# Attention, experts and MLP in one kernel: rooms of 240 rows in the wide expert stages, a rewritten end of attention, other pauses between scatters

## The chip, the cores and the metric

The kernel runs on one core of one Trainium2 chip. The time is device time in microseconds (us), from the start to the end of one execution. A profile of one execution gives the rows that are shown below; engines are PE (TensorE, matmuls), PEld (its weight loads), DVE (VectorE), ACT (ScalarE), POOL (GpSimd) and SP (SyncE, which issues most loads).

## The reference

Attention in a window of 64 feeds a mixture of experts, which feeds an MLP. Cut to what matters:

```python
# attention: q, k, v of shape (2, 8, 576, 64); tokens see themselves and 63 before
attn = softmax(q @ k.T / sqrt(64), masked to the window)
x = (attn @ v) as 1152 tokens x 512
# experts: 8 of them, each token goes to one
expert_idx = argmax(x @ w_gate);  gate_w = its probability
for i in range(1152):             # places in order, at most 288 per expert
    if counts[e := expert_idx[i]] < 288: disp[e, counts[e]] = x[i]; counts[e] += 1
y = relu(disp @ w1) @ w2          # 512 -> 1024 -> 512, per expert
out[i] = gate_w[i] * y[expert_idx[i], pos[i]]
# MLP on all 1152 tokens
h = out @ w_in                    # 512 -> 2048
g = max(h, 0) + alpha * min(h, 0)
return g @ w_out                  # 2048 -> 512
```

With the inputs used here the experts get 254, 234, 220, 194, 123, 74, 42 and 11 tokens, in order of size.

## The kernel before, in words

**Precision.** Big products are made from three fast ones. Each float32 operand is split into a high and a low half in the matmul type f32r (11 bits of mantissa): `whi` and `wlo` of the weights, `xh` and `xl` of the data; a product is whi·xh + wlo·xh + whi·xl. ACT makes most `whi` (each fourth is made by DVE), DVE makes all `wlo`. Some small products use plain float32 (`xap`, `aps`, `ay`, `pps`, `py`).

**Attention.** Nine tiles of 128 tokens go through a pipeline that is written out by hand: in turn `t`, PE makes the scores of tile t (`pe_scores`), transposes the probabilities of tile t-1 (`pe_turn`, tile `tp`; `put_turn` copies them out as `ptT`), multiplies them by the values (`pe_values`), and for tile t-2 transposes the result (`pe_columns`) and makes the gate's logits (`pe_logits`, tile `lg`). Engines run their instructions in the order of the code.

**Routing.** Tiles are routed in three batches: b0 is tiles 0 to 3, b1 tiles 4 to 6, b2 tiles 7 and 8. A batch goes through `choosing` (the best expert of each token), `weighing` (its probability), `pe_dispatch` and `dispatching` (each token's row number `sl` in the table), and then one `scatter` per tile: an indirect DMA on POOL that writes 128 rows of 528 words to a table `xe` in HBM, sorted by expert. These small steps on DVE are Python generators; `step(n)` puts n of b0's next steps between the steps of attention. Behind each scatter stand a memset of the tile `spacer` and five memsets of the tile `between`, which pace POOL.

**The star.** After b0 the kernel guesses the largest expert (`choose_star`) and takes the rows that it has so far: DVE makes one-hot matrices (`pick`), PE gathers with them (`pe_ahead`, tile `xap`), and its first 128 rows go through the expert in plain float32 (`go_ahead`: matmuls `aps`, transposes `atp`, matmuls `ay`), while the routing of b2 is under way. After the last scatter, `star_rows` gathers its other rows with one indirect DMA (`sx`). It waits for all scatters, and the stream of weight loads goes on behind it.

**Experts.** Experts are sorted by size, and a place p has the expert of rank `ORDER[p]`, ORDER = (0, 1, 4, 2, 5, 6, 7, 3). Each place has a room, a fixed number of rows:

```python
WIDE, NARROW, HALF = min(cap, 256), 128, 64
room = [WIDE if 1 <= r <= 3 else HALF if r >= 6 else NARROW for r in ORDER]
```

Places 1, 3 and 7 (`HOST`) are wide: tokens are the moving side of the matmul and 128 columns of the weights stand in the array. `wide_up` makes 96 matmuls into `hps`, ACT and DVE turn these into `hh` and `hl`; `wide_down` makes 96 matmuls into `y`, which go out as the halves `x2h`, `x2l`. Places 0, 2 and 4 are narrow: 128 tokens stand in the array and weights move (`sps` and `sy`; `sh`, `sl` and transposes `stp` between). Places 5 and 6 (`PAIR`) have 64 rows each and run in plain float32 between the steps of HOST. What each expert has beyond its room is handled behind a test that these inputs don't reach.

Rows reach the experts by indirect DMAs on POOL (`rows_of`): nine gathers `xg`, two for a wide place, and nine gathers `gt` of the gates.

**Loads.** SP streams weights into tiles `raw` as they come free; `prepare` splits the next weight tile wherever the stages call it. In the HOST stage the first weights of the MLP are converted too (`cvt_tick`: ACT's `mag`, DVE's `w`).

**MLP.** Four rounds, each on a quarter of the hidden columns for three blocks of 384 tokens: matmuls `gps` (384 columns) and `ops` (512 columns), with the PReLU on ACT and DVE between.

Of the kernel before, what the change touches and what calls it, by code (L numbers as in the profile page):

```python
# [27 lines left out]
def attention_moe_mlp_kernel(  # L28
# [27 lines left out]
    room = [WIDE if 1 <= r <= 3 else HALF if r >= 6 else NARROW for r in ORDER]  # L56
# [151 lines left out]
    spacer = const.tile([1, 1], F32, name="spacer")  # L208
# [13 lines left out]
    with tc.manual_schedule():  # L222
# [13 lines left out]
        with ExitStack() as es:  # L236
# [205 lines left out]
            def pe_turn(t):  # L442
                tps[t] = []
                for s in range(2):
                    tps[t].append(ps_t.tile([128, 4, 128], F32, name="tp", tag="tp"))
                    for p in range(4):
                        nc.tensor.transpose(tps[t][s][:, p, :], pts[t][s][:, p, :], identf)  # L447
                    if t == NTILE - 1 and not s:
                        pe_ahead((1,), b0[:2])

            def put_turn(t):
                ptTs[t] = []
                for s in range(2):
                    ptTs[t].append(wk.tile([128, 4, 128], F32, name="ptT", tag="ptT"))
                    (nc.vector.tensor_copy if s and t == NTILE - 1 else nc.scalar.copy)(ptTs[t][s], tps[t][s])
# [327 lines left out]
            def scatter(t, ts, sl):  # L783
# [5 lines left out]
                for _ in range(5):  # L789
# [130 lines left out]
            for t in range(NTILE + 2):  # L920
                if t < NTILE:
                    pe_scores(t)
                    if t < 2:
                        keep_busy(4 - t)
                    peak(t, int(t < NTILE - 1))
                    if t == NTILE - 1:
                        run(*chain)
                if 1 <= t <= NTILE:
                    if t == NTILE:
                        chosen, weights, places = choosing(b1), weighing(b1), dispatching(b1)  # L930
                        some(chosen, 6)
                        some(weights, 2)
                    if t == NTILE:
                        pe_ahead((0,))
                    pe_turn(t - 1)
                    put_turn(t - 1)
                if t == NTILE:
                    run(chosen)
                if t >= 2:
                    if t == NTILE + 1:  # L940
                        pe_ahead((1,), b0[2:])
                    pe_columns(t - 2)
                    put_columns(t - 2)
                if t == NTILE:
                    pe_dispatch(b1)
                    some(places, 8)
                if t < NTILE:
                    softmax(t, HEADS)
                if t == NTILE + 1:
                    pe_ahead((2,))  # L950
                    xa = wk.tile([128, 4, 128], F32, name="axT", tag="ptT")
                    nc.scalar.copy(xa[:, :2], star_x[0][:, :2])
                    run(places)
                    while waiting:
                        scatter(*waiting.pop(0))
                if 1 <= t <= NTILE:
# [3 lines left out]
                if 1 <= t <= NTILE:  # L960
# [3 lines left out]
                if t == NTILE:  # L964
                    run(weights)
                pe_free.append(t)
                step({6: 4, 7: 6}.get(t, 2))
# [3 lines left out]

            choose(b2)
            going = go_ahead()
            pe_ahead((3,))
            nc.scalar.copy(xa[:, 2:], star_x[0][:, 2:])
            pe_dispatch(b2)
            next(going)
            weigh(b2)

# [6 lines left out]
            while waiting:  # L986
                scatter(*waiting.pop(0))
# [30 lines left out]
        with ExitStack() as es:  # L1018
# [6 lines left out]
            def rows_of(dst, src, index):  # L1025
# [3 lines left out]
                for x in scattered:  # L1029
                    tc.add_manual_dep(ins.ins, x.ins.name, mybir.DependencyInfo(  # L1030
                        mybir.DependencyClass.Sync, mybir.DependencyReason.DATA), reason="rows scattered")

            def gather(p):

                for h in range(room[p] // 128 if p not in PAIR else 1):
# [40 lines left out]
            def wide_up(p, xt, between=lambda c: None):  # L1076
                hT, at = [], first_part[p]
                for c in range(4):
                    hi, lo = (w.rearrange("p (k f) -> p k f", k=4) for w in parts.pop(at + c))
                    ps = ps_h.tile([128, 2, WIDE], F32, name="hps", tag="h")  # L1080
                    for f in range(2):
                        fs = slice(128 * f, 128 * f + 128)

                        for n, (i, j) in enumerate(((0, 0), (1, 0), (0, 1))):
                            for kk in range(4):
                                nc.tensor.matmul(ps[:, f, :], (hi, lo)[i][:, kk, fs], xt[j][:, kk, :],  # L1086
# [5 lines left out]
                    hh = hp.tile([128, 2, WIDE], F32R, name="hh", tag="hh")  # L1092
# [467 lines left out]
```

## Time and profile before

| | us |
|---|---|
| median of 3 runs | 408.92 |
| their range | 408.39 to 409.47 |
| the profiled execution's own time | 407.18 |
| its span in the profile | 405.3 |
| mean granted TensorE clock, as a share of full speed | 0.992 |

The profiled execution is one more run, so its own time is not the median; its span runs from the first to the last instruction on the core. A row's durations come from this one execution. Where a row says x24, 24 instructions of a kind are taken together, and the time is theirs from the first start to the last end; matmuls overlap in the array, so the distance between two of them is such a time in the chain divided by the count, not the mean duration of one.

### The profile page before, as it was taken

What the parts mean: (1) busy time and instruction counts of PE and PEld (TensorE: products, weight loads), DVE (VectorE), ACT (ScalarE), POOL (GpSimd) and SP (SyncE); (2) the same over time, 40 slices, a digit from 0 to 9 for tenths busy, and PEclk for the clock granted to TensorE, in tenths of its full rate; (3) what the DMA queues carried; (4) which work ended last, traced back from release to release, by engine and by line L of the source; (5) the groups of instructions that cost most, each with busy time, mean ns of one, the idle gap of its engine ahead of it and who ended that gap; (6) DMA issues with size and microseconds to landing.
All of it is one profiled execution on the core that took longest, in us unless ns stands there. A gap on an engine that the chain in (4) does not pass through costs nothing.

```text
span 405.3 us, 7932 instructions
## 1 busy us (share of the span) xinstructions
PE 388.7 (96%) x2931; PEld 345.9 (85%) x2932; DVE 286.5 (71%) x686; ACT 198.2 (49%) x371; POOL 66.4 (16%) x170
## 2 busy tenths in 40 slices
PE   7999997999999999999999999999999999999991
PEld 4888873999989996877999889998899988999880
DVE  3779797689987765558599866999739972355220
ACT  4979464474563444453377655774127620254000
POOL 5542687010037100000000000000000000000431
PEclk9999999999999999999999999999999999999996
DMA  7761975999997572986323343323401000000221
GB/s 260 243 202 42 352 275 170 394 408 407 342 303 266 181 241 71 341 292 232 107 95 116 109 151 131 129 104 112 149 1 55 0 2 0 0 2 1 81 104 56
DMA packets 20446, 66.12 MB, mean 163 GB/s; under 512 B 2992, under 2 KB 2992, under 8 KB 20400
## 3 DMA queue, kind: packets, MB, share of 16 engines
q1 hardware_dynamic: 17728, 57.74, 40.5%
q0 software_dynamic: 2528, 7.53, 5.1%
q8 instruction: 25, 0.41, 0.4%
q10 hardware_dynamic: 144, 0.26, 0.2%
q14 instruction: 21, 0.17, 0.1%
HBM read 60.74 MB, written 4.79 MB: 162 GB/s over the span
## 4 chain that ended last, share of the span: by engine, by line
PE 87%; DVE 5%; DMA 3%; issue 2%; POOL 1%; ACT 1%; SPq 0%; POOLq 0%
PE gps L220 25%; PE ops L1387 24%; PE y L220 9%; PE hps L1086 7%; PE sps L220 4%; PE sy L220 4%; PE sc L419 2%; PE pps L1254 2%; PE py L1269 2%; PE av L463 2%; PE tp L447 1%; DMA v<-v_in 1%; PE lg L489 1%; DMA sx<-xe,ix 1%; PE xtp L1061 1%
## 5 line engine op out<-in xcount | busy, mean ns | idle before, releaser
L220 PE MATMUL gps<-x2h,wlo 128*128 128x384 f32 x192 | 64.2, 334 | 0.0
L220 PE MATMUL gps<-x2h,whi 128*128 128x384 f32 x192 | 64.2, 334 | 0.0
L220 PE MATMUL gps<-x2l,whi 128*128 128x384 f32 x192 | 64.2, 334 | 0.0
L144 DVE TENSOR_TENSOR wlo<-raw,whi 128x1024 fp32r<-128x1024 f32 x45 | 53.8, 1223 | 11.9 <-ACT whi L1070 10.8
L1363 ACT ACTIVATE u<-gps,one 128x384 f32<-128x384 f32 x48 | 27.7, 577 | 58.7 <-PE gps L220 58.7
L1387 PE MATMUL ops<-whi,gl 128*128 128x512 f32 x144 | 56.1, 390 | 0.0
L1387 PE MATMUL ops<-wlo,gh 128*128 128x512 f32 x144 | 56.1, 390 | 0.0
L1387 PE MATMUL ops<-whi,gh 128*128 128x512 f32 x144 | 56.0, 389 | 0.0
L1395 POOL DMA_INDIRECT out<-acc,tok x9 | 8.7, 965 | 254.9 <-DVE acc L1393 254.9
L1393 DVE SCALAR_TENSOR_TENSOR acc<-ops,gate,acc 128x512 f32<-128x512 f32 x27 | 20.0, 748 | 33.1 <-PE ops L1387 33.1
L1364 DVE SCALAR_TENSOR_TENSOR g<-gps,slope,u 128x384 f32<-128x384 f32 x48 | 29.4, 613 | 18.9 <-ACT u L1363 18.8
L220 PEld LDWEIGHTS gps<-x2h,whi 128*128 128x128 f32 x192 | 36.1, 188 | 0.1
L220 PEld LDWEIGHTS gps<-x2l,whi 128*128 128x128 f32 x192 | 36.1, 188 | 0.1
L220 PEld LDWEIGHTS gps<-x2h,wlo 128*128 128x128 f32 x192 | 36.0, 188 | 0.0
L1070 ACT CAST whi<-raw 128x1024 fp32r<-128x1024 f32 x30 | 31.0, 1048 | 10.0 <-PE y L220 9.6
L1374 ACT ACTIVATE gh<-g,sign 128x384 fp32r<-128x384 f32 x48 | 29.3, 611 | 9.6 <-DVE g L1364 9.6
L1387 PEld LDWEIGHTS ops<-whi,gl 128*128 128x128 f32 x144 | 27.0, 188 | 5.6
L1387 PEld LDWEIGHTS ops<-wlo,gh 128*128 128x128 f32 x144 | 27.0, 188 | 5.6
L1387 PEld LDWEIGHTS ops<-whi,gh 128*128 128x128 f32 x144 | 27.0, 188 | 5.5
L1375 DVE SCALAR_TENSOR_TENSOR gl<-g,sign,gh 128x384 fp32r<-128x384 f32 x48 | 29.2, 609 | 0.2 <-ACT gh L1374 0.2
L190 DVE TENSOR_TENSOR wlo<-w,whi 128x512 fp32r<-128x512 f32 x32 | 22.0, 687 | 9.4 <-ACT whi L189 9.4
L220 PE MATMUL y<-hh,whi 128*128 128x256 f32 x96 | 27.6, 288 | 0.0
(285 smaller groups left out, 815.4 us busy)
## 6 DMA issues: line engine op xcount, KB each, us to landing
raw<-moe_in SPq DMA_DIRECT2D x61, 512.0 KB
raw<-mlp_in SPq DMA_DIRECT2D x32, 512.0 KB
v<-v_in SPq DMA_DIRECT2D x8, 260.0 KB
sw<-moe_in SPq DMA_DIRECT2D x4, 512.0 KB
qT<-q_in SPq DMA_DIRECT2D x6, 256.0 KB
kT<-k_in SPq DMA_DIRECT2D x5, 256.0 KB
qT<-q_in SPq DMA_DIRECT2D x2, 384.0 KB
kT<-k_in SPq DMA_DIRECT2D x2, 384.0 KB
```

The costliest lines, as they stand in the source:

```text
L144: eng.tensor_tensor(lo, raws.pop(split[c]), hi.bitcast(F32), op=ALU.subtract)
L190: nc.vector.tensor_tensor(lo, w, hi.bitcast(F32), op=ALU.subtract)
L220: nc.tensor.matmul(ps, wa[i], xa[j], start=start and n == 0, stop=stop and n == 2)
L1070: (nc.vector.tensor_copy if c % 4 == 3 else nc.scalar.copy)(ring_tiles(c)[0], raws[split[c]])
L1086: nc.tensor.matmul(ps[:, f, :], (hi, lo)[i][:, kk, fs], xt[j][:, kk, :], start=n == kk == 0, stop=n == 2 and kk == 3)
L1363: nc.scalar.activation(out=u, in_=ps, func=AF.Copy, scale=one[:, ft:ft + 1])
L1364: nc.vector.scalar_tensor_tensor(g, ps, slope[:, ft:ft + 1], u, op0=ALU.mult, op1=ALU.max)
L1374: nc.scalar.activation(out=gh, in_=g, func=AF.Copy, scale=sg)
L1375: nc.vector.scalar_tensor_tensor(gl, g, sg, gh.bitcast(F32), op0=ALU.mult, op1=ALU.subtract)
L1387: nc.tensor.matmul(ps, a_[:, ts_], b_[:, f % 2, :], start=f == 0 and n == 0, stop=f == 3 and n == 2)
L1393: nc.vector.scalar_tensor_tensor(acc[:, tt, :], ps, sc, acc[:, tt, :], op0=ALU.mult, op1=ALU.add)
L1395: ins = nc.gpsimd.indirect_dma_start(out=out[:, :], out_offset=bass.IndirectOffsetOnAxis(ap=tok[:, tt:tt + 1].bitcast(U32), axis=0), in_=a ...
```

## The change

Four things are changed.

1. The rooms of the three wide places go from 256 to 240 rows; all `hps` and `y` matmuls, and the instructions that read them, become 240 columns wide. The gathers still bring 128 rows each.
2. Behind each scatter stand two memsets of `between` and no longer five; the tile `spacer` has 32 elements and no longer 1.
3. The last two turns of the attention loop are written out behind the loop, in another order. The star's `xap` matmuls stand behind b1's scatters and not among them, the second half of `ptT` of the last tile is copied by ACT and not by DVE, and b0's steps are placed otherwise (`step({6: 4, 7: 1, 8: 0})` for `step({6: 4, 7: 6})`, `step(4)` in the last turn, and the rest of b0's chain behind b1's choosing).
4. Behind each gather of `rows_of` (nine `xg`, nine `gt`; not `sx`) stand eight memsets of `spacer`.

```diff
@@ -53,7 +53,7 @@
     ORDER = (0, 1, 4, 2, 5, 6, 7, 3)
     HOST, PAIR = 7, (5, 6)
     WIDE, NARROW, HALF = min(cap, 256), 128, 64
-    room = [WIDE if 1 <= r <= 3 else HALF if r >= 6 else NARROW for r in ORDER]
+    room = [min(cap, (NARROW, 240, 240, 240, NARROW, NARROW, HALF, HALF)[r]) for r in ORDER]
     NS = 2 * NE + 1
     NB = NS + 4 * NE
     MARK = 2048.0
@@ -205,7 +205,7 @@
 
     scattered = []
 
-    spacer = const.tile([1, 1], F32, name="spacer")
+    spacer = const.tile([1, 32], F32, name="spacer")
 
     def apart(earlier, ins):
 
@@ -439,20 +439,18 @@
                     nc.scalar.activation(out=pts[t][s][:, p, :], in_=scs[t][s][:, p, :], func=AF.Exp,
                                          scale=-1.0, bias=nms[t][:, s, p:p + 1])
 
-            def pe_turn(t):
-                tps[t] = []
-                for s in range(2):
+            def pe_turn(t, halves=(0, 1)):
+                tps.setdefault(t, [])
+                for s in halves:
                     tps[t].append(ps_t.tile([128, 4, 128], F32, name="tp", tag="tp"))
                     for p in range(4):
                         nc.tensor.transpose(tps[t][s][:, p, :], pts[t][s][:, p, :], identf)
-                    if t == NTILE - 1 and not s:
-                        pe_ahead((1,), b0[:2])
 
             def put_turn(t):
                 ptTs[t] = []
                 for s in range(2):
                     ptTs[t].append(wk.tile([128, 4, 128], F32, name="ptT", tag="ptT"))
-                    (nc.vector.tensor_copy if s and t == NTILE - 1 else nc.scalar.copy)(ptTs[t][s], tps[t][s])
+                    nc.scalar.copy(ptTs[t][s], tps[t][s])
 
             def pe_values(t):
                 avs[t] = ps_a.tile([128, 2, 512], F32, name="av", tag="av")
@@ -786,7 +784,7 @@
                     out_offset=bass.IndirectOffsetOnAxis(ap=sl[:, t - ts[0]:t - ts[0] + 1].bitcast(U32), axis=0),
                     in_=xr[:, t, :], in_offset=None)
                 apart(scattered, ins)
-                for _ in range(5):
+                for _ in range(2):
                     nc.gpsimd.memset(between, 0.0)
                 return ins
 
@@ -917,74 +915,81 @@
                 yield from count_star()
                 yield from pick_star(ts, sl)
 
-            for t in range(NTILE + 2):
-                if t < NTILE:
-                    pe_scores(t)
-                    if t < 2:
-                        keep_busy(4 - t)
-                    peak(t, int(t < NTILE - 1))
-                    if t == NTILE - 1:
-                        run(*chain)
-                if 1 <= t <= NTILE:
-                    if t == NTILE:
-                        chosen, weights, places = choosing(b1), weighing(b1), dispatching(b1)
-                        some(chosen, 6)
-                        some(weights, 2)
-                    if t == NTILE:
-                        pe_ahead((0,))
+            last = NTILE - 1
+            for t in range(NTILE):
+                pe_scores(t)
+                if t < 2:
+                    keep_busy(4 - t)
+                peak(t, int(t < last))
+                if t == last:
+                    step(4)
+                if t >= 1:
                     pe_turn(t - 1)
                     put_turn(t - 1)
-                if t == NTILE:
-                    run(chosen)
                 if t >= 2:
-                    if t == NTILE + 1:
-                        pe_ahead((1,), b0[2:])
                     pe_columns(t - 2)
                     put_columns(t - 2)
-                if t == NTILE:
-                    pe_dispatch(b1)
-                    some(places, 8)
-                if t < NTILE:
-                    softmax(t, HEADS)
-                if t == NTILE + 1:
-                    pe_ahead((2,))
-                    xa = wk.tile([128, 4, 128], F32, name="axT", tag="ptT")
-                    nc.scalar.copy(xa[:, :2], star_x[0][:, :2])
-                    run(places)
-                    while waiting:
-                        scatter(*waiting.pop(0))
-                if 1 <= t <= NTILE:
+                softmax(t, HEADS)
+                if t >= 1:
                     pe_values(t - 1)
                 if t >= 2:
                     pe_logits(t - 2)
-                if 1 <= t <= NTILE:
+                if t >= 1:
                     put_values(t - 1)
                 if t >= 2:
                     put_logits(t - 2)
-                if t == NTILE:
-                    run(weights)
                 pe_free.append(t)
-                step({6: 4, 7: 6}.get(t, 2))
+                step({6: 4, 7: 1, 8: 0}.get(t, 2))
                 pe_free.clear()
                 if t == 5:
                     chain.append(route(b0))
 
+            def send():
+                while waiting:
+                    scatter(*waiting.pop(0))
+
+            chosen, weights, places = choosing(b1), weighing(b1), dispatching(b1)
+            some(chosen, 6)
+            some(weights, 2)
+            pe_turn(last, (0,))
+            pe_columns(last - 1)
+            pe_turn(last, (1,))
+            put_turn(last)
+            put_columns(last - 1)
+            run(chosen, *chain)
+            pe_values(last)
+            pe_dispatch(b1)
+            pe_logits(last - 1)
+            put_values(last)
+            put_logits(last - 1)
+            some(places, 8)
+            run(weights, places)
+            send()
+            pe_ahead((0,))
+            pe_columns(last)
+            put_columns(last)
+            pe_ahead((1,))
+            xa = wk.tile([128, 4, 128], F32, name="axT", tag="ptT")
+            nc.scalar.copy(xa[:, :2], star_x[0][:, :2])
+            pe_logits(last)
+            put_logits(last)
+
             choose(b2)
             going = go_ahead()
-            pe_ahead((3,))
+            pe_ahead((2,))
+            pe_ahead((3,), b0[:2])
+            pe_dispatch(b2)
+            pe_ahead((3,), b0[2:])
             nc.scalar.copy(xa[:, 2:], star_x[0][:, 2:])
-            pe_dispatch(b2)
             next(going)
             weigh(b2)
-
 
             tot = pps[b2[0]][:, len(b2), :]
             sorting = sort()
             for n, _ in enumerate(dispatching(b2)):
                 if n == 3:
                     next(sorting)
-            while waiting:
-                scatter(*waiting.pop(0))
+            send()
             ix0 = [star_index()]
             star_ins = star_rows()
             while not rows:
@@ -1029,10 +1034,12 @@
                 for x in scattered:
                     tc.add_manual_dep(ins.ins, x.ins.name, mybir.DependencyInfo(
                         mybir.DependencyClass.Sync, mybir.DependencyReason.DATA), reason="rows scattered")
+                for _ in range(8):
+                    nc.gpsimd.memset(spacer, 0.0)
 
             def gather(p):
 
-                for h in range(room[p] // 128 if p not in PAIR else 1):
+                for h in range(1 + (room[p] > NARROW)):
                     xg = cvt.tile([128, ROW], F32, name="xg", tag=("mag", "w")[turn[0] % 2])
                     turn[0] += 1
                     rows_of(xg, xe[:, :], ixe[:, h, p:p + 1])
@@ -1074,7 +1081,7 @@
             late = []
 
             def wide_up(p, xt, between=lambda c: None):
-                hT, at = [], first_part[p]
+                hT, at, n_ = [], first_part[p], room[p]
                 for c in range(4):
                     hi, lo = (w.rearrange("p (k f) -> p k f", k=4) for w in parts.pop(at + c))
                     ps = ps_h.tile([128, 2, WIDE], F32, name="hps", tag="h")
@@ -1083,16 +1090,17 @@
 
                         for n, (i, j) in enumerate(((0, 0), (1, 0), (0, 1))):
                             for kk in range(4):
-                                nc.tensor.matmul(ps[:, f, :], (hi, lo)[i][:, kk, fs], xt[j][:, kk, :],
+                                nc.tensor.matmul(ps[:, f, :n_], (hi, lo)[i][:, kk, fs], xt[j][:, kk, :],
                                                  start=n == kk == 0, stop=n == 2 and kk == 3)
                         while late and f:
                             late.pop(0)()
                         if f == 0:
                             prepare(at + c)
-                    hh = hp.tile([128, 2, WIDE], F32R, name="hh", tag="hh")
-                    hl = hp.tile([128, 2, WIDE], F32R, name="hl", tag="hl")
-                    nc.scalar.activation(out=hh, in_=ps, func=AF.Relu)
-                    nc.vector.scalar_tensor_tensor(hl, ps, 0.0, hh.bitcast(F32), op0=ALU.max, op1=ALU.subtract)
+                    hh = hp.tile([128, 2, WIDE], F32R, name="hh", tag="hh")[:, :, :n_]
+                    hl = hp.tile([128, 2, WIDE], F32R, name="hl", tag="hl")[:, :, :n_]
+                    nc.scalar.activation(out=hh, in_=ps[:, :, :n_], func=AF.Relu)
+                    nc.vector.scalar_tensor_tensor(hl, ps[:, :, :n_], 0.0, hh.bitcast(F32), op0=ALU.max,
+                                                   op1=ALU.subtract)
                     hT.append((hh, hl))
                     between(c)
                     prepare(at + c + 1)
@@ -1102,7 +1110,7 @@
 
             def wide_down(p, win, hT, between=lambda c: None):
                 at = first_part[p] + 4
-                ys = [ps_y.tile([128, WIDE], F32, name=f"y{d}", tag="y") for d in range(4)]
+                ys = [ps_y.tile([128, WIDE], F32, name=f"y{d}", tag="y")[:, :room[p]] for d in range(4)]
 
                 def part(c, f, d, hi, lo):
                     dd = slice(128 * d, 128 * d + 128)
...
```

The order of instructions shows the moves. On POOL, the end of the scatters of b2 and the first gathers behind them (`xe` is the scatter of 128 rows, `sx` the star's gather, `xg` and `gt` those of the experts). Before:

```order
L784 DMA xe<-xr,sl 1152x528
L215 MEMSET spacer 1x1
L790 MEMSET between 1x128 x5
L784 DMA xe<-xr,sl 1152x528
L215 MEMSET spacer 1x1
L790 MEMSET between 1x128 x5
L727 DMA sx<-xe,ix_1398 128x528
L1026 DMA xg<-xe,ixe 128x528 x9
L1026 DMA gt<-xe,ixt 128x8 x9
```

and with the change:

```order
L782 DMA xe<-xr,sl 1152x528
L215 MEMSET spacer 1x32
L788 MEMSET between 1x128 x2
L782 DMA xe<-xr,sl 1152x528
L215 MEMSET spacer 1x32
L788 MEMSET between 1x128 x2
L725 DMA sx<-xe,ix_1371 128x528
L1031 DMA xg<-xe,ixe 128x528
L1038 MEMSET spacer 1x32 x8
L1031 DMA xg<-xe,ixe 128x528
L1038 MEMSET spacer 1x32 x8
```

Three `between` fewer stand behind each scatter, and the gathers have eight memsets behind each.

On DVE, the end of b1's choosing and the begin of its dispatching (`oh`, `add` and `cum` are the chosen experts and their counts; `batch` is the first step of the dispatching; `size`, `ids` and `pick` are b0's star). Before:

```order
L556 TENSOR_TENSOR oh<-back,mv 128x24
L571 TENSOR_REDUCE add<-oh 128x8
L574 TENSOR_TENSOR cum<-cum,add 128x8
L455 COPY ptT<-tp 128x512
L617 TENSOR_TENSOR batch<-pp,found 128x8
L619 SCALAR_TENSOR_TENSOR upto<-z,batch 128x8
L623 TENSOR_TENSOR off<-upto,pp 128x8
```

and with the change, from the second row behind `cum` on:

```order
L683 COPY size<-gone 128x1
L691 CAST slf<-sl 128x4
L694 TENSOR_SCALAR ids<-num,seg 128x128
L698 TENSOR_SCALAR pick_1182<-ids,slf 128x128
L698 TENSOR_SCALAR pick_1184<-ids,slf 128x128
L698 TENSOR_SCALAR pick_1186<-ids,slf 128x128
L698 TENSOR_SCALAR pick_1188<-ids,slf 128x128
L467 TENSOR_SCALAR r<-av 128x8
L469 RECIPROCAL r<-r 128x8
L471 TENSOR_TENSOR xr<-av,r 128x2x4x64
L492 COPY lgs<-lg 128x8
L615 TENSOR_TENSOR batch<-pp,found 128x8
```

The copy `ptT` is gone from there, and b0's picks and the last tile's rows `xr` stand between `cum` and `batch`; before, the picks stood ahead of b1's choosing, and that `xr` behind b1's `sl`.

On PE, the last tile's transposes (`tp`) and the star's `xap`. Before:

```order
L489 MATMUL lg<-wg,xT 64x8 x8
L709 MATMUL xap<-pick_1097,xr 128x128
L709 MATMUL xap<-pick_1099,xr 128x128
L709 MATMUL xap<-pick_1101,xr 128x128
L709 MATMUL xap<-pick_1103,xr 128x128
L447 MATMUL tp<-identf,pt 128x128 x4
L709 MATMUL xap<-pick_1097,xr 128x128
L709 MATMUL xap<-pick_1099,xr 128x128
L447 MATMUL tp<-identf,pt 128x128 x4
L479 MATMUL tx<-identf,xr 128x128 x4
L595 LDWEIGHTS onesb
```

and with the change:

```order
L487 MATMUL lg<-wg,xT 64x8 x8
L447 MATMUL tp<-identf,pt 128x128 x4
L477 MATMUL tx<-identf,xr 128x128 x4
L447 MATMUL tp<-identf,pt 128x128 x4
L461 MATMUL av<-v_125,ptT 64x65
L461 MATMUL av<-v_127,ptT 64x65
```

The first six `xap` products, which stood around the last tile's transposes, are gone from there; all 16 now come behind b1's scatters.

## Rows read from the trace of the kernel before

**Rows 1.** the page: busy time, share and instructions; granted clock in 40 slices.

```profile
PE 388.7 (96%) x2931; PEld 345.9 (85%) x2932; DVE 286.5 (71%) x686; ACT 198.2 (49%) x371; POOL 66.4 (16%) x170
...
PEclk9999999999999999999999999999999999999996
```

**Rows 2.** the chain that ended last, in order of time: start us, us, what.

```profile
48.53 0.89 PE xap L709 x8
...
53.25 0.16 DVE xr L637
...
58.38 2.73 DMA xe<-xr,sl
...
61.90 4.01 DMA sx<-xe,ix
...
83.78 2.83 PE hps L1086 x24
...
95.96 11.51 PE y L220 x96
...
113.53 1.44 PE sy L220 x6
...
198.31 24.96 PE gps L220 x144
223.27 24.52 PE ops L1387 x108
```

**Rows 3.** PE's timeline: start us, us, instructions, [idle before <-releaser].

```profile
51.62 5.43 PE L765 MATMUL aps<-raw,axT 128*128 128x256 f32 x24
...
61.20 1.88 PE L776 MATMUL ay<-sw,axT 128*128 128x512 f32 x4
66.04 0.63 PE L739 MATMUL atp<-identf,sx 128*128 128x128 f32 x4 [2.96 <-DMA sx<-xe,ix]
...
129.60 0.74 PE L1086 MATMUL hps<-xwh,whi 128*128 128x256 f32 x4 [0.18 <-DVE hl L1095]
```

**Rows 4.** POOL's timeline, same columns.

```profile
48.87 0.96 POOL L784 DMA_INDIRECT xe<-xr,sl  x1 [1.92 <-DVE found L645]
49.83 0.09 POOL L215 MEMSET spacer<- 1x1 f32 x1
49.87 1.20 POOL L790 MEMSET between<- 1x128 f32 x5
...
58.38 0.97 POOL L784 DMA_INDIRECT xe<-xr,sl  x1 [0.17 <-issue]
...
63.77 1.93 POOL L1026 DMA_INDIRECT xg<-xe,ixe  x1 [0.30 <-issue]
...
133.05 0.94 POOL L1026 DMA_INDIRECT gt<-xe,ixt  x1 [0.30 <-issue]
```

**Rows 5.** DVE's timeline at the last tile of attention.

```profile
44.94 0.68 DVE L455 COPY ptT<-tp 128x512 f32<-128x512 f32 x1
```

**Rows 6.** windows: PE, PEld, DVE, ACT, POOL busy (instructions), PEclk, DMA, GB/s.

```profile
52.00:56.00 4.00, 4.00 (x20) 3.53 (x19) 3.55 (x29) 1.08 (x3) 3.22 (x14) 1.00 1.01 397
56.00:60.00 4.00, 4.00 (x20) 3.14 (x19) 3.69 (x16) 3.17 (x5) 3.48 (x12) 1.00 0.34 132
...
96.00:108.00 12.00, 12.00 (x102) 12.00 (x101) 11.86 (x16) 5.25 (x10) 0.94 (x1) 1.00 0.99 372
```

**Rows 7.** PE's groups by form: one of three hps forms.

```profile
L1086 PE MATMUL hps<-xwl,whi 128*128 128x256 f32 x96 | 15.2, 279 | 0.0
```

**Rows 8.** DVE's timeline behind the first wide stage.

```profile
103.40 3.50 DVE L144 TENSOR_TENSOR wlo<-raw,whi 128x1024 fp32r<-128x1024 f32 x3
...
108.86 1.22 DVE L144 TENSOR_TENSOR wlo<-raw,whi 128x1024 fp32r<-128x1024 f32 x1 [0.52 <-ACT whi L1070]
...
113.05 0.69 DVE L1183 TENSOR_TENSOR sl__2222<-stp,sh 128x512 fp32r<-128x512 f32 x1
```

**Rows 9.** the tile raw: idle before it (us, times), by releaser.

```profile
  DMA raw<-mlp_in: 3.0, 3
```

More of the change, by code (lines that the diff above doesn't have):

```diff
@@ L1151, in halves_of @@
             def halves_of(p):
-                tag = "xw" if room[p] == WIDE else "xt"
-                xt = [xtp.tile([128, 4, room[p]], F32R, name=f"{tag}{n}", tag=f"{tag}{n}") for n in "hl"]
+                tag, n_ = ("xw", WIDE) if room[p] > NARROW else ("xt", NARROW)
+                xt = [xtp.tile([128, 4, n_], F32R, name=f"{tag}{n}", tag=f"{tag}{n}")[:, :, :room[p]] for n in "hl"]
                 for h, tp in enumerate(turned(p)):
-                    hi, lo = (x[:, :, 128 * h:128 * h + 128] for x in xt)
+                    hi, lo = (x[:, :, 128 * h:min(room[p], 128 * h + 128)] for x in xt)
+                    tp = tp[:, :, :min(128, room[p] - 128 * h)]
                     nc.scalar.copy(hi, tp)
@@ L1325, in attention_moe_mlp_kernel @@
                     continue
-                elif room[p] == WIDE:
+                elif room[p] > NARROW:
                     hT = wide_up(p, xts.pop(p), lambda c: gather_gates() if (p, c) == (1, 1) else None)
```

## The prediction

> **What bounds the kernel now.** I read the page first, for one engine that is nearly always busy. TensorE (PE) is: 388.7 of 405.3 us, at a granted clock in the top tenth through nearly the whole span [rows 1]. So time is lost only where PE waits, and won only where PE's own work gets shorter. The chain of work that ended last says which work that is, in order of time. From 198.31 us on it is the second MLP alone, four rounds of gps and ops matmuls [rows 2]; the change does not touch them. Before that lie the experts, whose wide stages alternate hps and y matmuls; and before those the piece that is not PE: the last scatter's landing and the gather sx, which waits for all scatters. PE's timeline shows what that piece costs: PE has finished the first half of the star's ay matmuls at 61.20 + 1.88 = 63.08 us and stands idle 2.96 us, until sx lands [rows 3]. All later MoE work, the stream of weight loads too (it is tied to sx's issue), follows from that point. So there are two places to win: the start of the experts (at most the 2.96 us that PE waits there, since PE's own work before it stays) and the wide stages.
>
> **Shorter pauses and the new end of attention.** Five scatters follow one another on POOL: the first at 48.87, the last at 58.38 [rows 4], so (58.38 - 48.87) / 4 = 2.38 us apart. Between them stand five memsets of 1x128 in 1.20 us, about 0.25 each, of which three go: 0.75 a gap. The spacer grows from 1 to 32 elements. No row has that form; it lies between the 1x1, behind which the next memset starts 0.04 later (49.83, 49.87), and the 1x128 at 0.25, so it adds 0 to 0.2; I take 0.05, since 32 elements are nearer to 1 than to 128. That is 0.70 a gap and 4 x 0.70 = 2.8 us at the last scatter. The first of the five also comes earlier. POOL waited for it 1.92 us, for DVE's found of b1 [rows 4]. In the order of DVE the same instructions stand ahead of that found as before, b0's picks and the last tile's xr among them, only in another order, but for the copy of ptT, 0.68 us [rows 5], which goes to ScalarE (ACT, 198.2 us busy in the whole span [rows 1]). Of the 0.68 I take 0.4, since the last tile's xr now waits for PE ahead of b1's places and not behind them. Is the data ready for the earlier scatters? The last two need b2's rows, written to 53.25 + 0.16 = 53.41 us [rows 2]; the fourth scatter would come at about 48.5 + 3 x 1.68 = 53.5. Just so; with still shorter pauses they would wait for that.
>
> What speaks against the full 3.2 us is the landing. The last scatter landed 2.73 us after issue, at 61.11, in a stretch where the DMA engines were busy 0.34 [rows 2, 6]. At 55.2 it would be issued while they are busy 1.01, moving 397 GB/s. One more load of 512 KB ahead of it at that rate would take 524 KB / 397 GB/s = 1.3 us. So the landing costs 0 to 1.3 us more; I take 0.5, because only the last 0.8 us of that stretch are in its way. Start: 3.2 - 0.5 = **2.7 us**; bounds 4 x 0.55 + 0.4 - 1.3 = 1.3 and the cap, 2.96.
>
> The picks' xap matmuls that move behind b1's cost PE nothing new: as many as before, and PE has no idle from 52 to 60 either way [rows 6].
>
> **Rooms of 240.** Each of the three wide stages has 96 hps matmuls (288 in all, 96 of each of the three forms of which one stands in [rows 7]) and 96 y matmuls [rows 2]: 576 together. Successive matmuls of 256 columns stand 2.83 / 24 = 118 ns (hps) and 11.51 / 96 = 120 ns (y) apart [rows 2]. The same f32r form with more columns gives the slope: gps with 384 in 24.96 / 144 = 173 ns, ops with 512 in 24.52 / 108 = 227 ns, so (227 - 173) / 128 = 0.42 ns a column. From 256 to 384 the same slope holds ((173 - 119) / 128 = 0.42). Sixteen columns less are 6.7 ns, and 576 x 6.7 = **3.9 us**, if the line goes on below 256. No f32r matmul in this trace has fewer columns; that is the unknown of this part.
>
> The nearest thing that could stop the line is the loading of the 128 weight columns that each matmul brings. Pairs of 128 columns with 128 weight columns run at 0.89 / 8 = 111 ns (xap) [rows 2], so that loading fits in 111 ns, and 118 - 6.7 = 111. By the rows it just fits, and I count the whole 3.9.
>
> The Trainium skill (TensorE: Matmul & The Clock Gate, LDWEIGHTS (loading the stationary operand)) gives a load as its column count over 1.2, in ns, whatever the rows: 107 for 128 columns, and the section Back-to-back issue gap has the spacing set by both operations together. The row agrees as far as it goes, 111 and not less. Were the load and not the streaming the limit at 118, nothing would be won in the wide stages; that is the first rival below, worked out there from rows.
>
> **What is given back.** A shorter PE stage helps only if the engines that feed it keep up.
> First, behind the first wide stage. DVE is busy 11.86 of 12 us from 96 to 108 [rows 6]; three weight splits end at 106.90, and its only hole before it makes sl for PE is 0.52 us at 108.86 [rows 8]. sl ends at 113.05 + 0.69 = 113.74, and PE's third sy matmul, which needs it, stands at 113.53 + 2 x 0.24 = 114.0 [rows 2]: slack 0.26. The stage before gets shorter by 192 x 6.7 ns = 1.3, so 1.3 - 0.52 - 0.26 = **0.5 us** comes back as a wait at sy. Narrower puts on DVE (hl and x2l lose a sixteenth) could return up to 0.2 of it.
> Second, at 129.60 PE waits 0.18 us for hl already [rows 3]. Before it lie 72 hps of the second wide stage, 0.48 us of saving, and the DVE work that ends in this hl is released after only 24 of them, 0.16. So the wait grows by **0.3 us**.
> Third, the HOST stage: ACT waited there 3.0 us, in three waits, for the loads raw of the MLP's weights [rows 9]. Loads don't come earlier because PE is faster. Of the third stage's 1.3 us anything from 0 to 1.3 may be lost so; I take **0.7**, the middle.
> Wide stages: 3.9 - 0.5 - 0.3 - 0.7 = **2.4 us**, bounds 1.6 and 3.9.
>
> **Clearings.** Eight memsets of 1x32 behind each of 18 gathers, each at most the 0.25 us of a 1x128, so at most 2.0 us a gather on POOL. What is queued behind them is the next gather. The first one is issued at 63.77 [rows 4], and its user in the first wide stage stands ahead of hps at 83.78 [rows 2], 20 us later; two gathers and 4 us of clearings don't fill that. The last of the nine gates is issued at 133.05; with 9 x 2.0 = 18 us it is 151, and the gates are used in the HOST stage behind 160. Cost nothing; if a later gather's rows came late, each 2 us of clearing would cost PE that much.
>
> **Sum.** 2.7 + 2.4 = 5.1 us. The profiled execution's own time was 407.18 (span 405.3 and 1.9 around it), so such a run would give 402.1. The median of the runs shown is 408.92, 1.74 above; the same 5.1 us off it is **403.8**, my forecast, with a range of its own from 401.9 (2.96 + 3.9 + 0.2 off) to 405.6 (1.3 + 2.0 off).
>
> **Rivals.**
> *Weight loading sets the spacing.* Then hps and y stay at 118 to 120 ns, nothing is given back either, and only the start is won: 408.92 - 2.7 = 406.2. For it: 111 ns is the shortest pair of this shape in the trace, and 120 of y lies 2 ns over hps. Against: the line from 512 down to 256 columns shows no bend. Chance 0.14.
> *The start doesn't come.* The scatters go closer together into DMA engines that are busy 1.01, land no earlier, and sx waits as before: 408.92 - 2.4 = 406.5. For it: that stretch [rows 6]. Against: POOL went from scatter to scatter at the pace of its own memsets, in the same load [rows 4]. Chance 0.10.
> *Both are eaten.* DVE, the loads or a gather behind clearings hold PE wherever it gets ahead: about 408.9. For it: DVE's 11.86 of 12. Against: PE's two small waits are all that it shows in the experts now. Chance 0.10.
> *Below 256 columns f32r is slower.* No row has f32r with fewer than 256 columns. Plain f32 matmuls of 256 columns, aps, take 5.43 / 24 = 226 ns a record, of which each matmul has two [rows 3]. If the short form falls to one such pass at 240 columns, 226 x 240 / 256 = 212 ns, 93 more than 119: 576 x 93 ns = 54 us, about 460. With both passes 424 ns, 305 more: 176 us, about 582. It decides from 2.7 us / 576 = 4.7 ns a matmul on: a spacing over 124 ns makes the whole slower than before. Against: no bend in the line; for: every f32r matmul of the trace has at least 256 columns, so nothing excludes it. Chance 0.10.
>
> **How the numbers follow.** Forecast 0.56, rivals 0.14, 0.10, 0.10 and 0.10. A measurement here can tell about 0.3%, 1.2 us, from no change. Forecast and the first two rivals are faster: 0.80; the third is within: 0.10; the fourth is slower: 0.10. The range leaves out the last two, 2 in 10, and reaches to the first two: 401.9 to 407.0 (406.5 and half a us for the start's unknowns).
>
> **What would show it.** Right: five scatters about 1.7 us apart, the last at about 55.2; PE's wait for sx under 0.5 us with atp at about 63.3; hps and y at 111 to 113 ns; a new PE wait of about 0.5 us for sl after the first wide stage; the second MLP beginning at about 193.2. Wrong: hps still at 118 (first rival) or over 124 (fourth); sx's landing still near 65.9 (second); PE waits for xg, ACT or DVE in the wide stages that add up to over 3 us (third).

## The result and the profile after

| | before | with the change |
|---|---|---|
| median, us | 408.65 (6 runs, 406.16 to 409.47) | 403.24 (6 runs, 401.32 to 405.19) |
| ratio of the times | | 0.989, 95% interval 0.9861 to 0.9919 |
| the profiled execution's own time | 407.18 | 405.19 |
| its span | 405.3 | 403.4 |
| its mean granted clock | 0.992 | 0.988 |

The change is faster by 5.4 us in the medians and by 4.5 (3.3 to 5.7) by the ratio, and 403.24 stands beside the forecast of 403.8. One run of the kernel with the rooms alone, 412.02 us at a mean clock of 0.981, is left out of its median and ratio below. But the execution that was profiled happens to be the longest of the six, 2 us over their median, and it shows a step of the forecast failing. The page, parts 1 and 2:

```profile
PE 386.3 (96%) x2932; PEld 341.7 (85%) x2932; DVE 284.8 (71%) x685; ACT 197.9 (49%) x372; POOL 79.2 (20%) x287
...
PEclk9999998999999999999999999999999999999997
```

PE is still the bound, and one slice of the clock, the seventh, has lost a tenth against [rows 1]. The chain that ended last, in order of time, at the places of [rows 2]:

```profile
55.22 5.37 DMA xe<-xr,sl
...
61.38 4.36 DMA sx<-xe,ix
...
66.50 5.13 PE ay L774 x8
...
85.28 2.68 PE hps L1093 x24
...
133.06 10.75 PE y L220 x96
...
195.99 25.39 PE gps L220 x144
```

The last scatter is issued 3.16 us earlier (55.22 for 58.38), but it takes 5.37 us to land where it took 2.73, so sx goes out only 0.52 us earlier (61.38 for 61.90). Then ay takes 5.13 us, and the wide stages begin at 85.28, which is 1.50 *later* than before. From there on all is gain: 24 hps take 2.68 us (112 ns each, 118 before), 96 y 10.75 (112 for 120), and the second MLP begins at 195.99, 2.32 earlier than before. So in this execution the wide stages gave 3.8 and the start took 1.5; of the 3.8 the first gps round gives 0.43 back (25.39 for 24.96). PE's timeline, as [rows 3]:

```profile
60.22 1.88 PE L774 MATMUL ay<-sw,axT 128*128 128x512 f32 x4
65.88 0.63 PE L737 MATMUL atp<-identf,sx 128*128 128x128 f32 x4 [3.77 <-DMA sx<-xe,ix]
...
129.67 0.71 PE L1093 MATMUL hps<-xwh,whi 128*128 128x240 f32 x4 [0.42 <-DVE hl L1102]
```

PE finished its work ahead of sx 0.98 earlier than in [rows 3] (60.22 for 61.20), and so waited 3.77 us and not 2.96. The new end of attention freed it sooner in this execution; it does not in each, as the next run shows. The windows behind that wait (columns as in [rows 6]):

```profile
66.00:68.00 2.00, 2.00 (x7) 0.97 (x7) 0.69 (x1) 1.46 (x3) 1.56 (x7) 0.61 0.61 148
68.00:70.00 2.00, 2.00 (x4) 0.92 (x3) 1.84 (x2) 1.02 (x2) 1.73 (x4) 0.54 1.01 356
70.00:72.00 2.00, 2.00 (x9) 1.09 (x8) 1.93 (x15) 0.33 (x1) 1.44 (x10) 1.00 0.95 330
```

For about 4 us the granted clock was 0.61 and 0.54, at or near the lower of its two levels (1.2 GHz), and back at the higher after that. That is why ay, plain work of a known length, took 5.13 us; before, with the clock at 1.00, the chain has it at 3.44:

```profile
66.67 3.44 PE ay L776 x8
```

POOL's timeline, as [rows 4]:

```profile
48.61 0.97 POOL L782 DMA_INDIRECT xe<-xr,sl  x1 [4.37 <-DVE found L643]
49.58 0.11 POOL L215 MEMSET spacer<- 1x32 f32 x1
49.64 0.45 POOL L788 MEMSET between<- 1x128 f32 x2
...
55.22 0.97 POOL L782 DMA_INDIRECT xe<-xr,sl  x1 [0.17 <-issue]
...
64.67 1.32 POOL L1038 MEMSET spacer<- 1x32 f32 x8
```

The scatters stand (55.22 - 48.61) / 4 = 1.65 us apart, as worked out (1.68), and eight clearings take 1.32 us.

### The profile page after: what moved, and what is told of

It reads as the page before. It is cut to its first block, busy times and chain, and to the rows that moved or that the text cites. A ratio compares the mean times of both kernels' runs of the same rounds, so it can differ in the third digit from the quotient of the medians.

```text
span 403.4 us, 8048 instructions
## 1 busy us (share of the span) xinstructions
PE 386.3 (96%) x2932; PEld 341.7 (85%) x2932; DVE 284.8 (71%) x685; ACT 197.9 (49%) x372; POOL 79.2 (20%) x287
## 4 chain that ended last, share of the span: by engine, by line
PE 83%; DMA 7%; DVE 3%; issue 2%; ACT 2%; SPq 1%; POOL 0%; POOLq 0%; DVEq 0%
PE gps L220 25%; PE ops L1396 24%; PE y L220 7%; PE hps L1093 7%; PE sy L220 4%; DMA v<-v_in 3%; PE sps L220 3%; PE pps L1263 2%; PE py L1278 2%; PE av L461 1%; DMA xe<-xr,sl 1%; PE sc L419 1%; PE ay L774 1%; DMA kT<-k_in 1%; DMA sx<-xe,ix 1%
## 5 line engine op out<-in xcount | busy, mean ns | idle before, releaser
L189 ACT CAST whi<-w 128x512 fp32r<-128x512 f32 x32 | 19.6, 612 | 16.4 <-DVE w L177 16.4
```

What stands on the lines that cost most here:

```text
L189: nc.scalar.copy(hi, w)
```

## The experiments

Two theories stood after this. Theory 1 is that on record. Theory 2: the scatters' landing is set by the DMA engines, which work off the loads queued there, so the start is worth nothing, and the wide stages give all they have. The twelve kernels ran in three batches, each on a chip of its own and beside its own runs of the kernel before. The medians of those are 407.87 (the change again, rooms alone, all but the rooms, pauses alone), 407.39 (no pauses, the new end alone, without the clearings, the three smaller rooms) and 408.28 (the two with rooms and pauses, the two with empty matmuls). The behaviour of one kernel is read from one profiled execution.

**The change again.** No edit.

> The changed kernel once more, for its profile. The theory on record (theory 1: the earlier scatters bring sx and the experts 2.7 us forward, the wide stages net 2.4) expects 5.1 us off and, in the profile, PE waiting for sx under 1 us. The theory formed on the first profile after the change (theory 2: the last scatter lands when the DMA engines have drained, near 60.6 whenever it is issued, so the start is worth about nothing, and the wide stages give all of their 3.9 us) expects about 4 us off, the landing of the last scatter 5 us behind its issue and PE waiting for sx 3.5 to 4 us again.

Measured: 402.84 us, ratio 0.9882 (0.9851 to 0.9913). From its chain, POOL's and PE's timelines:

```profile
56.47 3.60 DMA xe<-xr,sl
...
82.56 2.68 PE hps L1093 x24
```

```profile
49.86 0.97 POOL L782 DMA_INDIRECT xe<-xr,sl  x1 [6.20 <-DVE found L643]
```

```profile
61.95 1.88 PE L774 MATMUL ay<-sw,axT 128*128 128x512 f32 x4
64.86 0.63 PE L737 MATMUL atp<-identf,sx 128*128 128x128 f32 x4 [1.02 <-DMA sx<-xe,ix]
65.32 3.17 PE L774 MATMUL ay<-sw,axT 128*128 128x512 f32 x7
```

The wait for sx is 1.02 here and the clock stays at 1.00: the 1.5 us lost in the first profile are not in every execution. Its hps begin at 82.56, 1.22 earlier than before. The same kernel behaves otherwise ahead of sx than in the first profile: b1's first scatter comes at 49.86 and not at 48.61, since POOL waits longer for b1's found, the last one is issued at 56.47 and not at 55.22, and PE starts its last ay at 61.95, later than before (61.20) and not earlier. Theory 1 is too high for the start, theory 2 too low.

**Rooms alone.** `room` and the widths of 240, on the kernel before.

> Only the rooms of 240, all else as before. Theory 1: 2.4 us off the kernel before. Theory 2: 3.9 us off, with hps and y 111 to 112 ns apart and waits of PE in the wide stages as before, or a few tenths longer.

Measured: 404.89 us, ratio 0.9937 (0.9909 to 0.9966): 2.6 us off by the ratio (1.4 to 3.7), 3.0 in the medians. That fits theory 1's 2.4; theory 2's 3.9 lies just outside the interval.

**All but the rooms.** The change with `240` replaced by `256`.

> The whole change but the rooms, which stay at 256: pauses, end of attention and clearings. Theory 1: 2.7 us off. Theory 2: within 0.5 us of the kernel before, or up to 1.5 slower where PE's longer wait for sx lowers its clock.

Measured: 406.13 us, ratio 0.9961 (0.9936 to 0.9986): 1.7 us off, between the theories. Theory 2's "nothing" falls.

**Pauses alone**, on the kernel before.

```diff
-    spacer = const.tile([1, 1], F32, name="spacer")
+    spacer = const.tile([1, 32], F32, name="spacer")
-                for _ in range(5):
+                for _ in range(2):
                     nc.gpsimd.memset(between, 0.0)
```

> Only the pauses (two memsets of between, spacer of 32), all else as before. Theory 1: 2.1 to 2.8 us off. Theory 2: within 0.5 us; the scatters come 1.7 us apart and the last lands no earlier than 60.5.

Measured: 406.0 us, ratio 0.9952 (0.993 to 0.9975): 1.9 us off, as much as pauses, new end and clearings together. Its chain:

```profile
55.12 3.99 DMA xe<-xr,sl
...
59.90 4.26 DMA sx<-xe,ix
...
82.00 2.83 PE hps L1086 x24
...
118.73 2.83 PE hps L1086 x24
...
142.87 4.24 PE sps L220 x36
...
196.53 24.96 PE gps L220 x144
...
246.02 24.98 PE gps L220 x144
```

The last scatter is 3.26 earlier than in [rows 2], its landing 1.26 longer (3.99 for 2.73), sx 2.00 earlier, hps 1.78 earlier. The rest of this kernel runs as before, 196.53 for 198.31 at the first gps.

**No pauses at all**, on the kernel before: the loop over `between` left out, the spacer of 32.

> The kernel before with no memset of between at all and the spacer of 32: scatters 1.2 us apart. If the pace of POOL still bounds the start, the last scatter is issued at 53.5 or a little later (b2's rows are ready at 53.4) and the time is 0.7 to 1.3 us less than with two memsets, about 405. If the landing behind the loads bounds it, the last scatter lands between 58.7 and 59.2 as with two memsets, and the time stays at 406.

Measured: 406.21 us, ratio 0.9959 (0.9933 to 0.9984), the same as with two memsets. Its chain:

```profile
54.60 6.42 DMA xe<-xr,sl
61.80 3.77 DMA sx<-xe,ix
```

Issued earlier still, the last scatter took 6.42 us and landed at 61.02 (in an execution of 407.21 us, 1.0 over the median). The issue was no longer at POOL's pace either: the last scatter but one waited 0.91 us for DVE, at the end of b2's routing. Over all profiles in whose chain its landing shows, the last scatter lands between 58.8 and 61.1, whether it is issued at 54.3 or at 58.4. So below two pauses POOL's pace no longer bounds the start; the landing does. That it waits there for the loads fits the busy share of the DMA engines, and is not shown by a run with other loads: with the pauses alone the share is 0.76 from 56 to 58 us and 0.06 from 58 to 60, and the scatter lands at 59.11; without pauses it is 1.00 and 0.58, and it lands at 61.02.

**The new end of attention alone**: the hunks of the diff from `pe_turn` to `send()`, with five pauses, spacer of 1, rooms of 256, no clearings.

> Only the new end of attention, with five pauses, the old spacer, rooms of 256 and no clearings. Theory 1 (on record): the copy that leaves DVE brings b1's first scatter and with it everything 0.4 us forward. Theory 3 (formed on the runs so far: with the new end b1's found came 1.0 to 1.5 us later than with the old one in two of three profiles, and the pauses alone gained as much as pauses, new end and clearings together): 0.5 to 1.0 us slower than before, b1's first scatter 12.5 to 13.5 us behind b0's first and not 11.6.

Measured: 410.61 us, ratio 1.006 (1.0036 to 1.0085): slower, by 2.4 us by the ratio and 3.2 in the medians. The cause that was expected is not the one found: b1's first scatter came at 48.69, earlier than before. Its chain, PE's timeline and the windows:

```profile
62.66 4.44 DMA sx<-xe,ix
...
87.41 2.83 PE hps L1091 x24
```

```profile
60.29 1.88 PE L774 MATMUL ay<-sw,axT 128*128 128x512 f32 x4
67.23 1.08 PE L737 MATMUL atp<-identf,sx 128*128 128x128 f32 x4 [5.06 <-DMA sx<-xe,ix]
68.11 5.62 PE L774 MATMUL ay<-sw,axT 128*128 128x512 f32 x8
```

```profile
66.00:68.00 2.00, 0.77 (x4) 0.80 (x5) 0.00 (x0) 0.00 (x0) 1.47 (x2) 0.50 0.74 218
68.00:70.00 2.00, 2.00 (x5) 0.96 (x4) 0.72 (x2) 1.65 (x3) 1.36 (x2) 0.50 0.85 206
70.00:72.00 2.00, 2.00 (x4) 0.82 (x3) 2.00 (x2) 0.83 (x1) 0.00 (x0) 0.50 0.96 334
```

PE is done with its work ahead of sx 0.91 earlier than before (60.29 for 61.20), as in the first profile of the change, while sx comes 1.19 later (67.23 for 66.04 at atp; it goes out at 62.66 for 61.90). PE waits 5.06 us, and the clock is at its lower level (0.50) for six us behind that. The wide stages begin at 87.41 for 83.78: of these 3.63 us, 1.19 come from the later sx, and 2.44 from atp and ay at the lower clock (6.50 us for 4.06). Why sx came later is not shown. The mean granted clock of all twelve runs lies between 0.984 and 0.987; with the pauses alone, where PE waited 1.55, all twelve lie at 0.991 or more.

**The change without the clearings.**

> The whole change without the clearings. Theory 1: the clearings cost nothing and bring nothing, so 402.8 to 403.3 as the whole change. Rival: the clearings hold later gathers, and without them it is faster by 0.5 us or more; or they keep POOL's gathers out of the way of the loads, and without them it is slower by as much.

Measured: 404.64 us, ratio 0.9928 (0.9899 to 0.9957). It looks 1.8 slower than the change run again, but the intervals overlap and the chip is another one. The clock is a rival to the clearings as well: ten of these twelve runs have a mean clock of 0.984 to 0.988, and four of the six of the change run again have 0.992 or more. See the next pair.

**Rooms and pauses, without and with clearings**, both on the old end of attention.

> Rooms of 240 and the short pauses on the kernel before, with its old end of attention and no clearings. If the new end only costs (theory 3: it lets PE finish its work ahead of sx earlier, PE waits longer for sx, and the granted clock is lower behind that wait), this is as fast as the whole change or faster by up to 1.5 us: 401.5 to 403, with PE's wait for sx at 1 to 2 us, the clock 1.00 from 66 to 84, and a mean clock of 0.991 or more in nearly all runs. If the new end is needed for the gain with 240 (theory 1), it is slower than the whole change, 404 or more.

> The same with the eight clearings behind each gather. If clearings cost and bring nothing, the same time as without, within 0.5 us. If they are what made the whole change faster than it is without them (402.8 against 404.6 measured), 1 to 2 us less.

Measured on one chip: 403.09 us without, ratio 0.9884 (0.9849 to 0.9919), and 402.48 with, 0.9859 (0.983 to 0.9888). Rooms and pauses alone are as fast as the whole change; the rest of the diff is not needed for the gain. The clearings differ by 0.6 us within overlapping intervals. In the two profiles the wide stages begin at 82.02 and 82.01 and the second gps round at 243.04 and 242.88, so neither a gain nor a cost shows there. The chain of the kernel without clearings, beside that of the pauses alone, gives the rooms stage by stage:

```profile
55.02 4.66 DMA xe<-xr,sl
...
82.02 2.68 PE hps L1086 x24
...
117.55 2.68 PE hps L1086 x24
...
140.55 4.25 PE sps L220 x36
...
171.02 4.64 DMA raw<-mlp_in
...
193.02 0.44 PE gps L220
193.46 25.06 PE gps L220 x143
...
243.04 24.98 PE gps L220 x144
```

and its PE timeline has the waits:

```profile
126.44 0.71 PE L1086 MATMUL hps<-xwh,whi 128*128 128x240 f32 x4 [0.41 <-DVE hl L1095]
...
193.02 0.44 PE L220 MATMUL gps<-x2h,whi 128*128 128x384 f32 x1 [0.17 <-ACT x2h L1113]
193.46 0.44 PE L220 MATMUL gps<-x2l,whi 128*128 128x384 f32 x1
193.74 0.34 PE L220 MATMUL gps<-x2h,wlo 128*128 128x384 f32 x1
```

**Empty matmuls in the wait for sx**, on the whole change (8 of them) and on rooms and pauses (5).

```diff
             def star_rest():
+                keep_busy(8)
                 tp = turned(star_x[1])
```

> The whole change, with eight empty bf16 matmuls of 512 columns on PE (their result is read by nobody) between the star's last ay and the wait for sx, about 1.8 us of work. If the lower clock behind the wait costs time, the mean clock is 0.991 or more in nearly all runs, ay behind the wait takes 3.4 to 3.6 us in every profile, and the time is 1 to 1.5 us less than the whole change's. If the clock doesn't matter there, the time is the same or up to 0.8 longer where sx comes before the matmuls end.

> Rooms of 240 and the short pauses on the old end, no clearings, with five such empty matmuls (1.1 us) in the wait for sx. If theory 3 is right the clock is already kept there, and they change nothing within 0.5 us; if the clock still falls now and then, the highest times go and the median falls by up to 1 us.

Measured: 403.21 us, ratio 0.988 (0.9843 to 0.9917), and 402.9, 0.9867 (0.9839 to 0.9896): no gain over the same kernels without them. In the first one's profile PE waits no more ahead of atp (at 64.93) and ay runs at full clock, but two of its six runs still have a mean clock of 0.986 and 0.987, and those are its longest (405.8 and 403.69). So the lower clock behind sx is real where it shows, but these runs do not show that it sets the median of the whole change. It is not the only place where the clock falls either: in the profile of all but the rooms it is 0.73, 0.50 and 0.91 in the three windows from 42 to 48 us, at the end of attention, and 1.00 behind sx.

**Rooms of 240, 224 and 208.**

```diff
-    room = [min(cap, (NARROW, 240, 240, 240, NARROW, NARROW, HALF, HALF)[r]) for r in ORDER]
+    room = [min(cap, (NARROW, 240, 224, 208, NARROW, NARROW, HALF, HALF)[r]) for r in ORDER]
```

> The whole change, with rooms of 240, 224 and 208 in the three wide places (enough for 234, 220 and 194 tokens). By the line of 0.42 ns a column hps and y stand 105 ns apart at 224 and 98 at 208, 3.9 us less work of PE than with 240, of which perhaps 2 to 3 us stay: 400 to 401. If the loading of 128 weight columns sets a floor near 107 to 111 ns, they stay at 107 to 112 at 224 and 208 alike, and the time gets less by 0 to 1.9 us at most: 401 to 403. Third, if short f32r matmuls fall to another rate somewhere below 240, far slower.

Measured: 404.1 us, ratio 0.9914 (0.9883 to 0.9945), no better than 240. Its PE timeline in the stage of 208 columns:

```profile
163.74 0.61 PE L1093 MATMUL hps<-xwh,wlo 128*128 128x208 f32 x4
164.19 0.61 PE L1093 MATMUL hps<-xwl,whi 128*128 128x208 f32 x4
164.64 0.61 PE L1093 MATMUL hps<-xwh,whi 128*128 128x208 f32 x4
```

Four matmuls start every 0.45 us: 112 ns each, the same as with 240 (112). The line of 0.42 ns a column would give 98. The floor is there. It is read from this spacing; the time alone would not settle it, since eight of the nine runs have a mean clock of 0.985 to 0.989.

## Why the prediction came out right

The time, 403.24 for 403.8, and the direction are right. Of its two terms one was too high and one too low, and they nearly cancelled; that the sum came so close is in part luck. A slip in it has no effect: the wide stages' lower bound is 1.6 where it is worked out and 2.0 in the forecast's own range.

**The start, 2.7 predicted; 1.9 in the time with the pauses alone, 1.8 in that profile.** The issue was right with the old end of attention: scatters 1.65 us apart, the last at 54.6 to 55.1 (55.2 predicted). The new end makes it uncertain, 55.22 in the first profile of the change and 56.47 in the second. The failed step is the landing, "0 to 1.3 us more; I take 0.5": it took 1.26 more with the pauses alone (3.99), 1.93 with rooms and pauses (4.66) and 2.64 in the first profile of the change (5.37), the last two beyond the upper bound. The bound was made from one load that could stand in front. The run without pauses shows that it is the wrong kind of bound: the landing comes at 59 to 61 whatever the issue time, and what is issued earlier than with two memsets brings nothing (406.21 and 406.0 us). PE's wait for sx, forecast under 0.5 us, was 0.54 at the least where no empty matmuls filled it. The rival "the start doesn't come" was thus half right, and it had 0.10.

**The new end of attention, 0.4 predicted as a gain.** Alone it costs 2.4 by the ratio, 3.2 in the medians. The sum held that "PE's own work before it stays", and took PE's wait of 2.96 as the cap; the new end changes just that, and in two ways. Seven profiles have it. In four (the first of the change, the new end alone, the change without clearings, the three smaller rooms) b1's first scatter comes 11.1 us behind b0's first, for 11.6 before: the 0.4 is there. But PE starts its last ay ahead of sx 22.7 us behind b0's first scatter, for 23.9 before, waits 2.54 to 5.06 us for sx, and the granted clock falls to 0.50 to 0.54 around that wait in all four. In the other three (the change again, all but the rooms, the change with empty matmuls) b1's first scatter comes 12.3 to 13.3 us behind b0's, that ay 24.3 to 25.5, PE waits 1.02 at most, and the clock is 1.00 behind sx. What decides between the two is not shown.

The lower clock was no term at all. With short pauses the cost of the new end is mostly gone: 1.7 off with the new end and clearings, 1.9 without.

**The wide stages, 2.4 predicted; 2.6 with the rooms alone.** The rooms on top of the pauses, in their two profiles, give it term by term. Nominal: (2.83 - 2.68) x 4 hps quarters and 11.51 - 10.75 for y are 1.36 us a stage, 4.1 in three, for 3.9. First give-back (sl behind the first wide stage), 0.5 predicted: from hps to hps the profiles take 36.73 and 35.53, 1.20 less, so 0.16 came back. This term was mis-sized. Second (hl), 0.3: the wait grew from 0.18 to 0.41, and 1.36 - 1.14 = 0.22 came back up to sps. Third (HOST), 0.7: up to the first gps 1.19 of 1.36 stays, and the first gps and ops round takes 50.02 for 49.49 us, so 0.17 + 0.53 = 0.7. It fell where it was argued, at the loads, but not as a wait inside HOST: the first three gps stand 0.44 and 0.28 apart instead of 0.17, which is 0.38 of the 0.53 (the rest is at no one place). They stand behind x2h and x2l that wait on DVE and ACT for the conversion of the MLP's first weights, and the chain leads from those to the load raw of mlp_in at 171.02. Altogether 4.1 - 1.1 = 3.0 net.

**Weight loading, rival at 0.14.** As a rule for 240 it failed: hps and y went to 112. As a floor it holds just below. The line ends at 111 to 112 ns; at 224 and 208 columns nothing more is won. xap has the same 111 with 128 weight columns [rows 2], but that says less than the prediction took from it: xap is plain float32, and aps, plain float32 too, takes 226 ns a record for 256 columns [rows 3], so for xap's 128 the streaming alone could make 113. The loading of 128 weight columns is the likely cause of the floor; it is not shown, since no f32r matmul was tried with fewer of them. The Trainium skill (TensorE: Matmul & The Clock Gate, LDWEIGHTS (loading the stationary operand)) gives a load as its column count over 1.2 in ns, an estimate of 107 for 128 columns. The spacing measured here is 112, so the measured one is to be used.

**Short f32r matmuls, rival at 0.10.** Excluded down to 208 columns. **Clearings**, nothing predicted: nothing shown, and a gain of up to 1.8 us is neither shown nor excluded.

## What to carry to other kernels

Shortening the issue of transfers pays only until their landing is the limit (here three memsets fewer brought 1.9 us, and two more nothing); look at where a transfer lands in several profiles, not at its latency in one. Work that is moved ahead of a wait which stays where it is only lengthens the wait, and behind it TensorE may come back at half clock: in the profile of the new end alone that took 2.4 us. When a matmul's columns are cut, use the slope from longer ones, and try one step further than is planned: 112 ns was the floor, and cutting past 240 columns bought nothing.

## What was not expected of the hardware

The granted clock differs from execution to execution of one kernel. In the last batch the kernel before ran in 406.96 to 407.6 us where the mean clock was 0.992, and in 408.23 to 410.52 where it was 0.987 to 0.989. Around PE's wait for sx the clock fell to 0.50 to 0.54 in five profiles (waits of 2.54, 2.67, 3.01, 3.77 and 5.06 us) and stayed at 1.00 in others (among them 1.02, 1.55, 2.93 and 2.96 us), so the length of the wait alone does not tell them apart. What lowers it elsewhere, and in single runs of the other kernels, stays open.
